# Columns of a sliding-attention and shift-MLP kernel by transposing transfers out of SBUF

## The chip, the cores and the metric

The kernel runs on one core of one Trainium2 chip. The metric is the device time of one execution in microseconds; a lower time is better. The engines are named as the profile names them: PE is TensorE's matmul, PEld its weight load, DVE is VectorE, ACT is ScalarE, POOL is GpSimd, and SP is SyncE, which issues nearly all transfers.

## The reference

The input is x of 2048 rows by 512 columns. Two branches start from its layernorm, and the second gates the first:

```python
xn = _layernorm(x)
s  = A(xn, wqkv, wo)          # 32 heads of 16; each row attends to itself and 7 earlier rows, 2 apart
g  = silu(B(xn, w1, w2, w3, w4))
out = x + s * g

# B, with F = 1376
h   = gelu(layernorm(xn) @ w1)
hs  = concat(four 128-column quarters of h, shifted by +1, -1, +2, -2 rows) @ w2
x1  = xn + hs
B   = x1 + gelu(layernorm(x1) @ w3) @ w4
```

Note that B normalises xn, which is normalised already. The kernel keeps one column-wise copy of xn for q, k and v, and reaches the second normalisation by multiplying that copy with one factor for each row.

## The kernel before, in words

**Layout.** The rows are split by parity: `xn[0]` holds the even rows and `xn[1]` the odd ones, 1024 each. There are four chunks of 512 rows, of which 0 and 1 are even and 2 and 3 odd. A chunk lies in SBUF as four tiles of 128 rows by 512 columns. A matmul over the 512 columns needs the chunk column-wise, that is with columns on the partitions: `xnT[p]` holds xn that way, `xn2T` the same times the row factors, and `x1nT` the normalised x1 ahead of w3.

**Three ways of getting columns.** `turn` (L296) makes 8 TensorE transposes for two tiles into one PSUM bank, and VectorE copies it out (L303); chunks 1, 2 and 3 take two of these each, 16 transposes a chunk. Chunk 0 goes partly by `turn_one`. `columns` (L443), ahead of w3, is the other way: after the normalisation of a chunk it writes 512x512 to `x1n_dram` (L446) and reads it back with one transposing transfer (L450).

**Row factors.** `rows2` computes 512 factors, as 128 partitions by 4. They have to stand on every partition as a row. For chunks 1 and 2, `rows2_spread` (L264) turns the 128x4 on TensorE (L266), copies it on VectorE (L268), writes it to `r2_d` (L269) and reads it back, repeated over the 128 partitions (L271), into `xn2T`. For chunks 0 and 3, `rows2_here` (L273) makes a diagonal on VectorE (L277) and multiplies it with ones on TensorE (L282). Then `scaled` (L288) multiplies the columns with them on VectorE.

**Order.** All instructions are pinned in the order of the program on each engine; nothing is moved by a planner. So the order below L489 is the schedule, and each engine, and SP's queue, takes its own instructions in that order and waits at each for what it needs. `q_all`, `k_all`, `v_pair`, `w1`, `w2` and `w3` are the projections of one chunk: 16, 16, 8, 16, 16 and 44 matmuls of width 512 (`w1` is called by halves of 8, `v_pair` by two tiles). They take PSUM in pairs of banks, three pairs in turn, and ScalarE or VectorE must have read a pair before it is written again; `k_all` has four ScalarE evictions (L354), since each key is written twice, masked for even and odd heads. `w2(c)` adds the result to xn and takes the statistics of the second layernorm (`Norm`), `columns(c)` follows, and `w3(c)` reads `x1nT`. `w2(0)` needs hT of the even chunks 0 and 1 and of the odd chunk 2, for the shifts cross from one parity to the other. Weights are loaded by SP: w3 (1376 KB) behind the first row factors, w4 behind those of chunk 2. After w3 of all chunks comes a loop of 18 attention blocks mixed with the matmuls of w4 (L878), which the change doesn't touch.

Of the kernel before, what the change touches and what calls it, by code (L numbers as in the profile page):

```python
# [8 lines left out]
AF = mybir.ActivationFunctionType  # L9
ALU = mybir.AluOpType  # L10
BF16 = mybir.dt.bfloat16
# [3 lines left out]
def ap_of(base, dims, off=0):  # L15

    return bass.AP(base.tensor, base.offset + off, dims)
# [3 lines left out]
def kernel(  # L21
# [17 lines left out]
    PE, DVE, ACT, POOL, SP = nc.tensor, nc.vector, nc.scalar, nc.gpsimd, nc.sync  # L39

    def pin(ins):

        return tc.keep_in_program_order(ins)

    P = 128
    S = 2048
    D = 512
    F = 1376
    ND = D // P
# [4 lines left out]
    CH = 512  # L54
    NCH = S // CH
# [40 lines left out]
    def single():  # L96
        cnt["s"] += 1
        return PS[:, 6 + (cnt["s"] - 1) % 2, :]
# [54 lines left out]
    m57 = const.tile([P, QB], BF16, name="m57")  # L153
    e_sb = const.tile([P, 8, 8, 16], BF16, name="e_sb")
    zero = const.tile([P, D], BF16, name="zero")

    def head_masks():
        pin(DVE.tensor_reduce(
# [36 lines left out]
    hT = [b8([P, ND, M + 2], f"hT{p}") for p in range(2)]  # L195
    kM = [kbp.tile([P, ND, MK, 2], BF16, name=f"kM{p}", tag="kM") for p in range(2)]
    v_d = [dram.tile([MK, 2, D], BF16, name=f"v_d{p}") for p in range(2)]
    r2_d = dram.tile([NCH, CH], BF16, name="r2_d")
    x1n_dram = dram.tile([S, D], BF16, name="x1n_dram")
    vst = [b4([P, 2, 2, D], f"vst{i}") for i in range(2)]  # L200


# [4 lines left out]
    def small_t(name, shape, dt=F32):  # L207
        return small.tile(shape, dt, name=name, tag=name)
# [39 lines left out]
    def rows2(c, ln):  # L248

        r2 = small_t("r2", [P, TPC])  # L250
        r2b = small_t("r2b", [P, TPC], BF16)
        eng = DVE if c == 0 else POOL
        pin(eng.tensor_tensor(out=r2, in0=ln.rstd, in1=ln.rstd, op=ALU.mult))
        pin(eng.tensor_tensor(out=r2, in0=r2, in1=ln.mv[:, :, 1], op=ALU.mult))
        if c == 0:
            pin(ACT.activation(r2, r2, AF.Sqrt, bias=eps_t[:]))
            with nc.allow_low_precision("bf16 row factors"):
                pin(DVE.reciprocal(out=r2b, in_=r2))
        else:
            rsqrt_eps(r2, r2)  # L260
            pin(POOL.tensor_copy(out=r2b, in_=r2))
        r2s[c] = r2b

    def rows2_spread(c):  # L264
        pt = single().bitcast(BF16)[0:TPC, 0:P]
        pin(PE.transpose(pt, r2s[c], ident[:]))  # L266
        t = small_t("r2t", [TPC, P], BF16)
        pin(DVE.tensor_copy(out=t, in_=pt))  # L268
        pin(SP.dma_start(out=r2_d[c].rearrange("(j q) -> j q", q=P), in_=t))  # L269
        xn2Ts[c] = b4([P, ND, CH], "xn2T")  # L270
        pin(SP.dma_start(out=xn2Ts[c][:, ND - 1, :], in_=r2_d[c : c + 1, :].to_broadcast([P, CH])))  # L271

    def rows2_here(c):  # L273

        xn2Ts[c] = t = b4([P, ND, CH], "xn2T")
        d = t[:, 0, :].rearrange("p (j q) -> p j q", q=P)
        pin(DVE.tensor_tensor(  # L277
            out=d, in0=ident.unsqueeze(1).to_broadcast([P, TPC, P]), in1=r2s[c].unsqueeze(2).to_broadcast([P, TPC, P]),
            op=ALU.mult,
        ))  # L280
        pt = single()
        pin(PE.matmul(pt, lhsT=ones_bf[:], rhs=t[:, 0, :], start=True, stop=True))  # L282
        if c == 0:
            pin(ACT.activation(t[:, ND - 1, :], pt, AF.Copy))
        else:
            pin(DVE.tensor_copy(out=t[:, ND - 1, :], in_=pt))

    def scaled(c):  # L288
        p, k = c // 2, c % 2
        t = xn2Ts[c]  # L290
        pin(DVE.tensor_tensor(
            out=t, in0=xnT[p][:, :, k * CH : (k + 1) * CH],
            in1=t[:, ND - 1, :].unsqueeze(1).to_broadcast([P, ND, CH]), op=ALU.mult,
        ))

    def turn(c, h):  # L296
        p, k = c // 2, c % 2
        i = k * TPC + 2 * h
        pt = single().bitcast(BF16).rearrange("p (a j q) -> p a j q", a=ND, j=2)
        for j in range(2):  # L300
            for dt in range(ND):
                pin(PE.transpose(pt[:, dt, j, :], xn[p][:, i + j, dt * P : (dt + 1) * P], ident[:]))  # L302
        pin(DVE.tensor_copy(  # L303
            out=xnT[p][:, :, i * P : (i + 2) * P], in_=pt.rearrange("p a j q -> p a (j q)")
        ))

    def turn_one(c, t):
        p, k = c // 2, c % 2
        i = k * TPC + t
        pt = single().bitcast(BF16)[:, 0 : ND * P].rearrange("p (a q) -> p a q", a=ND)  # L310
        for dt in range(ND):
            pin(PE.transpose(pt[:, dt, :], xn[p][:, i, dt * P : (dt + 1) * P], ident[:]))
        pin(ACT.activation(xnT[p][:, :, i * P : (i + 1) * P], pt, AF.Copy))

    def q_half(pts, lo, hi, nts=range(ND)):
        for nt in nts:
# [28 lines left out]
    def k_pad(p):  # L345
        pin(POOL.memset(kM[p][:, :, 0:8, :], 0.0))
        pin(POOL.memset(kM[p][:, :, M + 8 : MK, :], 0.0))

    def k_all(c, parts=(0, 1)):
        p, k = c // 2, c % 2  # L350
        for a in parts:
            pt = proj(c, a, wqk_sb[:, :, D : 2 * D], chunk(xnT, c))
            for e in range(2):
                pin(ACT.activation(  # L354
                    kM[p][:, 2 * a : 2 * a + 2, 8 + k * CH : 8 + (k + 1) * CH, e], pt, AF.Copy, scale=em[:, e : e + 1]
                ))
# [29 lines left out]
    def v_pair(p, t):  # L386
        pt = pair()
        for i in range(2):
            v_mm(p, t + i, pt[:, i, :])
        v_keep(p, t, 2, pt[:, 0, :])  # L390

    def v_pad(p):
        rows = v_d[p].rearrange("r e d -> (r e) d")
        pin(SP.dma_start(out=rows[0:16], in_=zero[0:16, :]))
        pin(SP.dma_start(out=rows[2 * (M + 8) : 2 * MK], in_=zero[0:4, :]))

    def w1(c, a):
        p, k = c // 2, c % 2
        pt = proj(c, a, w1_sb, xn2Ts[c])
        pin(ACT.activation(  # L400
            hT[p][:, 2 * a : 2 * a + 2, 1 + k * CH : 1 + (k + 1) * CH], pt, AF.Gelu_apprx_tanh
        ))
# [12 lines left out]
    def w2(c, order="a0 s0 a1 s1"):  # L415

        p, k = c // 2, c % 2
        x_c = x_of(c)
        ln = ln2[c] = Norm(x_c, b4([P, TPC, D], "xn3"), TPC, "l3")
        pts = []  # L420
        for h in range(TPC // 2):
            pt = pair()
            pts.append(pt)
            for j in range(2):
                m0 = k * CH + (2 * h + j) * P
                for g in range(ND):
                    pin(PE.matmul(  # L427
                        pt[:, j, :], lhsT=w2_src(p, g, m0), rhs=w2_sb[:, g, :],
                        start=(g == 0), stop=(g == ND - 1),
                    ))  # L430
        for what, i in (w for w in order.split()):
            if what == "a":
                h = int(i)
                xs = x_c[:, 2 * h : 2 * h + 2, :]
                pin(DVE.tensor_tensor(out=xs, in0=pts[h], in1=xs, op=ALU.add))  # L435
            elif what == "s":
                h = int(i)
                ln.stats(2 * h, 2 * h + 2)
            else:
                columns(c - 1)  # L440
        ln.root()

    def columns(c):  # L443
        ln = ln2[c]
        ln.apply(0, TPC)
        pin(SP.dma_start(  # L446
            out=x1n_dram[c * CH : (c + 1) * CH, :].rearrange("(i q) d -> q i d", q=P), in_=ln.dst
        ))
        x1nT = b4([P, ND, CH], "x1nT")
        pin(SP.dma_start_transpose(out=x1nT, in_=x1n_dram[c * CH : (c + 1) * CH, :]))  # L450
        x1nTs[c] = x1nT

    h3a, h3b = {}, {}
# [35 lines left out]
    for p in range(2):  # L489
        pin(POOL.memset(hT[p][:, :, 0:1], 0.0))  # L490
        pin(POOL.memset(hT[p][:, :, M + 1 : M + 2], 0.0))
        pin(POOL.memset(qT[p][:, :, M:MQ], 0.0))
    pin(POOL.memset(zero, 0.0))
    k_pad(0)
    k_pad(1)
    pin(ACT.activation(
# [32 lines left out]
    for a in range(2):  # L529
# [10 lines left out]
    v_pair(0, 2)  # L540
    k_all(0, (1,))
    v_pad(0)
    w1(0, 0)
    rows2_spread(1)
    pin(SP.dma_start(out=w3_sb, in_=B_w3.rearrange("(dt q) f -> q dt f", q=P)))
    turn(1, 0)
    turn(1, 1)
    w1(0, 1)
    l2 = Norm(x_of(2), x_of(2), TPC, "l1")
    l2.stats(0, 4)  # L550
    l2.root()
    l2.apply(0, 4)
    rows2(2, l2)
    l3 = Norm(x_of(3), x_of(3), TPC, "l1")
    l3.stats(0, 4)
    l3.root()
    scaled(1)
    q_all(1)
    k_all(1)
    v_pair(0, 4)  # L560
    l3.apply(0, 4)
    rows2(3, l3)
    v_pair(0, 6)
    rows2_spread(2)
    w1(1, 0)
    turn(2, 0)
    turn(2, 1)
    w1(1, 1)
    scaled(2)
    q_all(2)  # L570
    turn(3, 0)
    turn(3, 1)
    k_all(2)
    pin(SP.dma_start(
        out=w4_sb[:, 0 : NF - 1, :],
        in_=B_w4[0 : (NF - 1) * P, :].rearrange("(ft q) n -> q ft n", q=P),
    ))
    pin(SP.dma_start(out=w4_sb[0:FL, NF - 1, :], in_=B_w4[(NF - 1) * P : F, :]))
    rows2_here(3)
    scaled(3)  # L580
    w1(2, 0)
    w1(2, 1)
    w1(3, 0)
    w1(3, 1)
    w2(0)
    columns(0)
    v_pad(1)
    q_all(3)
# [403 lines left out]
```

## Time and profile before

| what | value |
|---|---|
| median of three runs | 199.26 us (197.72, 199.69, 199.26) |
| the profiled execution's own time | 197.26 us |
| its span in the profile | 195.5 us, mean granted clock 0.996 |
| PE busy | 185.5 us, 95% of the span |
| ACT busy | 133.3 us, 68% |
| DVE busy | 117.8 us, 60% |
| POOL busy | 19.1 us, 10% |
| transfers | 28.12 MB, mean 144 GB/s |
| start to the end of w3 | 0 to 112.4 us |
| attention blocks with w4 | 112.4 to 185 us |

The span is the time between the first and the last thing that the profiler saw; the execution's own time is 1.76 us longer. A busy share is an average over the span, so it says which engine is filled most, and a window of time says whether it is filled where the change is made. The chain that ended last is followed back from the end of the program: each piece of it is work, or a wait, that something later depended on.

### The profile page before, as it was taken

How to read it: one execution, taken by the hardware profiler on the slowest of the kernel's cores; microseconds unless marked ns; L12 is line 12 of the kernel's file. 1: busy time of each engine (PE TensorE's matmuls, PEld its weight loads, DVE VectorE, ACT ScalarE, POOL GpSimd, SP SyncE). 2: the span in 40 equal slices, each digit the busy share in tenths (PEclk: the TensorE clock that was granted, in tenths of full speed). 3: DMA queues.
4: the chain of work that ended last, by engine and by line, in shares of the span. 5: the costliest groups of instructions: out<-in, count | busy, mean ns of one | idle time of the engine just before them, and what ended most of it. 6: DMA issues, size and time to landing. Idle time of an engine off the chain costs nothing.

```text
span 195.5 us, 5255 instructions
## 1 busy us (share of the span) xinstructions
PE 185.5 (95%) x2253; PEld 91.8 (47%) x2283; DVE 117.8 (60%) x229; ACT 133.3 (68%) x151; POOL 19.1 (10%) x57
## 2 busy tenths in 40 slices
PE   7899999999999999999999999999999999999990
PEld 2474544554444444444444444445444544554540
DVE  5785767236076697494200035556487888798894
ACT  7399769649817615435656588877887876887871
POOL 3006066100002022006000000000000000000000
PEclk9999999999999999999999999999999999999998
DMA  4997480654000433752480051457565556582523
GB/s 131 339 368 239 132 282 15 218 158 157 0 0 3 136 83 109 215 107 65 110 260 0 0 162 60 157 166 232 153 216 161 137 155 215 127 247 51 171 91 126
DMA packets 33576, 28.12 MB, mean 144 GB/s; under 512 B 10760, under 2 KB 32528, under 8 KB 33552
## 3 DMA queue, kind: packets, MB, share of 16 engines
q1 hardware_dynamic: 33408, 27.71, 47.2%
q8 instruction: 18, 0.29, 0.6%
q10 hardware_dynamic: 144, 0.07, 0.1%
q14 instruction: 6, 0.05, 0.1%
HBM read 17.01 MB, written 8.67 MB: 131 GB/s over the span
## 4 chain that ended last, share of the span: by engine, by line
PE 85%; DMA 5%; DVE 4%; issue 2%; SPq 1%; ACT 1%
PE PS L469 19%; PE PS L328 19%; PE PS L764 19%; PE PS L427 5%; PE PS L811 4%; PE PS L795 4%; PE PS L652 3%; DMA wqk_sb<-in_A_wqkv_dram 3%; PE PS L626 3%; PE PS L362 3%; DMA x1nT<-x1n_dram 2%; PE PS L318 2%; PE PS L662 2%; PE PS L302 2%; DVE sg L825 2%
## 5 line engine op out<-in xcount | busy, mean ns | idle before, releaser
L469 PE MATMUL PS<-x1nT,w_sb 128*128 128x512 bf16 (+1 forms) x173 | 38.2, 379 | 0.4 <-DMA x1nT<-x1n_dram 0.3
L633 ACT ACTIVATE prob<-PS 128x1824 bf16<-128x1824 f32 x18 | 30.4, 1688 | 4.4 <-PE PS L626 3.6
L764 PE MATMUL PS<-w_sb,h3a 128*128 128x512 bf16 x112 | 29.2, 379 | 1.9 <-issue 1.7
L475 ACT ACTIVATE h3a<-PS 128x1024 bf16<-128x1024 f32 x16 | 16.4, 1024 | 21.0 <-PE PS L469 19.1
L777 DVE TENSOR_TENSOR xn<-PS,xn 128x512 bf16<-128x512 f32 x15 | 10.3, 686 | 32.0 <-PE PS L764 31.8
L469 PEld LDWEIGHTS <-w_sb 128*128 128x128 bf16 (+1 forms) x176 | 17.5, 100 | 20.9 <-issue 0.7
L328 PE MATMUL PS<-xnT,wqk_sb 128*128 128x512 bf16 x109 | 25.0, 379 | 0.2
L354 ACT ACTIVATE kM<-PS,em 128x1024 bf16<-128x1024 f32 x16 | 20.8, 1404 | 3.2 <-PE PS L328 3.2
L638 DVE TENSOR_TENSOR prob<-prob,maskb 128x1824 bf16<-128x1824 bf16 x18 | 19.8, 1102 | 1.8 <-ACT prob L633 1.8
L764 PEld LDWEIGHTS <-h3a 128*128 128x128 bf16 x128 | 11.3, 97 | 13.4 <-issue 1.2
L328 PEld LDWEIGHTS <-wqk_sb 128*128 128x128 bf16 x112 | 10.9, 98 | 12.8
L435 DVE TENSOR_TENSOR xn<-PS,xn 128x1024 bf16<-128x1024 f32 x8 | 9.6, 1213 | 11.3 <-PE PS L427 11.3
L811 PE MATMUL PS<-wo_sb,oT 128*128 128x512 bf16 (+1 forms) x68 | 15.5, 366 | 0.0
L328 PE MATMUL PS<-xn2T,w_sb 128*128 128x512 bf16 x62 | 14.6, 379 | 0.1
L427 PE MATMUL PS<-w_sb,hT 128*128 128x512 bf16 x63 | 14.4, 379 | 0.1
L821 ACT ACTIVATE sg<-PS 128x512 bf16<-128x512 f32 (+1 forms) x17 | 9.6, 572 | 6.1 <-PE PS L811 6.1
L764 PE MATMUL PS<-w_sb,h3b 128*128 128x512 bf16 (+1 forms) x44 | 12.8, 380 | 0.8 <-issue 0.8
L339 ACT ACTIVATE qT<-PS 128x1024 bf16<-128x1024 f32 x8 | 8.1, 1024 | 7.6 <-PE PS L328 7.6
L373 ACT ACTIVATE vst<-PS 128x512 bf16<-128x512 f32 (+1 forms) x12 | 8.8, 743 | 3.5 <-ACT sig L784 2.3
L221 DVE BATCH_NORM_STATS2 l1s<-xn 128x6 f32<-128x512 bf16 x16 | 10.1, 680 | 1.6 <-DMA xn<-in_A_x_dram 1.6
L400 ACT ACTIVATE hT<-PS 128x1024 bf16<-128x1024 f32 x8 | 8.1, 1031 | 3.8 <-PE PS L328 3.8
L221 DVE BATCH_NORM_STATS2 l3s<-xn 128x6 f32<-128x512 bf16 x16 | 10.2, 682 | 0.2
(105 smaller groups left out, 229.2 us busy)
## 6 DMA issues: line engine op xcount, KB each, us to landing
ring<-v_d SPq DMA_DIRECT2D x18, 256.0 KB, 3.3
v_d<-vst SPq DMA_DIRECT2D x16, 256.0 KB, 2.7
x1n_dram<-xn SPq DMA_DIRECT2D x4, 512.0 KB
xo<-in_A_x_dram SPq DMA_DIRECT2D x8, 256.0 KB, 4.1
ring<-rec_d SPq DMA_DIRECT2D x4, 456.0 KB, 4.7
out_dram<-xo SPq DMA_DIRECT2D x7, 256.0 KB
xn<-in_A_x_dram SPq DMA_DIRECT2D x6, 256.0 KB, 7.9
w_sb<-in_B_w_dram SPq DMA_DIRECT2D x1, 1376.0 KB
```

Source lines behind the costliest of these rows:

```text
L221: pin(DVE.bn_stats(out=self.st[:, j, :], in_=self.src[:, j, :]))
L328: pin(PE.matmul(pt[:, b, :], lhsT=w[:, dt, nt * P : (nt + 1) * P], rhs=rhs[:, dt, :], start=(dt == 0), stop=(dt == ND - 1),))
L354: pin(ACT.activation(kM[p][:, 2 * a : 2 * a + 2, 8 + k * CH : 8 + (k + 1) * CH, e], pt, AF.Copy, scale=em[:, e : e + 1]))
L427: pin(PE.matmul(pt[:, j, :], lhsT=w2_src(p, g, m0), rhs=w2_sb[:, g, :], start=(g == 0), stop=(g == ND - 1),))
L435: pin(DVE.tensor_tensor(out=xs, in0=pts[h], in1=xs, op=ALU.add))
L469: pin(PE.matmul(pt[:fs, ft % 2, :], lhsT=w3_sb[:, dt, ft * P : ft * P + fs], rhs=x1nT[:, dt, :], start=(dt == 0), stop=(dt == ND - 1),))
L475: pin(ACT.activation(t[:, o : o + 2, :], pt, AF.Gelu_apprx_tanh))
L633: pin(ACT.activation(pr, S_ps[:, :, 0 : ND * NQ], AF.Exp, scale=SCALE))
L638: pin(DVE.tensor_tensor(out=f, in0=f, in1=maskb[:], op=ALU.min))
L764: pin(PE.matmul(pt, lhsT=h3_of(c, ft)[:fs, jj * P : (jj + 1) * P], rhs=w4_sb[:fs, ft, :], start=(ft == 0), stop=(ft == NF - 1 and silu < 2),))
L777: pin(DVE.tensor_tensor(out=x_i, in0=pt, in1=x_i, op=ALU.add))
L811: pin(PE.matmul(pt[:, 0:W], lhsT=oT[p][:, dt, i * P : (i + 1) * P], rhs=wo["sb"][:, dt, c], start=(dt == 0), stop=(dt == ND - 1),))
```

## The change

The columns of chunks 2 and 3 no longer come by `turn` but by `turn_dma`: four transposing transfers for each chunk, 128x512 each, straight from xn in SBUF to `xnT` in SBUF. `columns` does the same with the normalised tiles: four transposing transfers out of SBUF for a chunk in place of a write to DRAM and one transposing transfer back.

The row factors of chunks 1, 2 and 3 are turned by VectorE: the 128x4 factors stand in a zeroed 128x32 tile (`r2p`), VectorE turns it in blocks of 32x32, and the result is written to DRAM as 128 pieces of 32 elements, so that the first 512 elements are the row. Write and read are two functions now, called at different places of the order; chunk 3 goes this way too, and no longer by `rows2_here`.

In the order, `l3.apply` and `rows2(3)` move ahead of the value projections, the load of w3 moves from behind the first row factors to behind the last, and `w2(0)` moves ahead of `w1(3, 1)`.

```diff
+    r2p = const.tile([P, NCH, 32], BF16, name="r2p")
...
-    r2_d = dram.tile([NCH, CH], BF16, name="r2_d")
-    x1n_dram = dram.tile([S, D], BF16, name="x1n_dram")
+    r2_d = dram.tile([NCH, 32 * P], BF16, name="r2_d")
...
             rsqrt_eps(r2, r2)
-            pin(POOL.tensor_copy(out=r2b, in_=r2))
+            r2b = r2p[:, c, :]
+            pin(POOL.tensor_copy(out=r2b[:, 0:TPC], in_=r2))
...
-    def rows2_spread(c):
-        pt = single().bitcast(BF16)[0:TPC, 0:P]
-        pin(PE.transpose(pt, r2s[c], ident[:]))
-        t = small_t("r2t", [TPC, P], BF16)
-        pin(DVE.tensor_copy(out=t, in_=pt))
-        pin(SP.dma_start(out=r2_d[c].rearrange("(j q) -> j q", q=P), in_=t))
+    def rows2_write(c):
+        t = small_t("r2t", [P, 32], BF16)
+        pin(DVE.transpose(out=t, in_=r2s[c]))
+        pin(SP.dma_start(out=ap_of(r2_d[c], [[32, P // 32], [P, 32], [1, 32]]), in_=t))
+
+    def rows2_read(c):
         xn2Ts[c] = b4([P, ND, CH], "xn2T")
-        pin(SP.dma_start(out=xn2Ts[c][:, ND - 1, :], in_=r2_d[c : c + 1, :].to_broadcast([P, CH])))
+        pin(SP.dma_start(out=xn2Ts[c][:, ND - 1, :], in_=r2_d[c : c + 1, 0:CH].to_broadcast([P, CH])))
...
+    def turn_dma(c):
+        p, k = c // 2, c % 2
+        for t in range(TPC):
+            i = k * TPC + t
+            pin(SP.dma_start_transpose(out=xnT[p][:, :, i * P : (i + 1) * P], in_=xn[p][:, i, :]))
...
         ln.apply(0, TPC)
-        pin(SP.dma_start(
-            out=x1n_dram[c * CH : (c + 1) * CH, :].rearrange("(i q) d -> q i d", q=P), in_=ln.dst
-        ))
         x1nT = b4([P, ND, CH], "x1nT")
-        pin(SP.dma_start_transpose(out=x1nT, in_=x1n_dram[c * CH : (c + 1) * CH, :]))
+        for t in range(TPC):
+            pin(SP.dma_start_transpose(out=x1nT[:, :, t * P : (t + 1) * P], in_=ln.dst[:, t, :]))
...
     v_pad(0)
+    rows2_write(1)
     w1(0, 0)
-    rows2_spread(1)
-    pin(SP.dma_start(out=w3_sb, in_=B_w3.rearrange("(dt q) f -> q dt f", q=P)))
     turn(1, 0)
     turn(1, 1)
+    rows2_read(1)
     w1(0, 1)
...
     l2.apply(0, 4)
+    turn_dma(2)
     rows2(2, l2)
...
     l3.root()
+    rows2_write(2)
     scaled(1)
     q_all(1)
     k_all(1)
+    l3.apply(0, 4)
+    turn_dma(3)
+    rows2_read(2)
+    rows2(3, l3)
+    rows2_write(3)
     v_pair(0, 4)
-    l3.apply(0, 4)
-    rows2(3, l3)
     v_pair(0, 6)
-    rows2_spread(2)
+    rows2_read(3)
+    pin(SP.dma_start(out=w3_sb, in_=B_w3.rearrange("(dt q) f -> q dt f", q=P)))
     w1(1, 0)
-    turn(2, 0)
-    turn(2, 1)
     w1(1, 1)
     scaled(2)
     q_all(2)
-    turn(3, 0)
-    turn(3, 1)
     k_all(2)
+    scaled(3)
...
-    rows2_here(3)
-    scaled(3)
     w1(2, 0)
     w1(2, 1)
     w1(3, 0)
+    w2(0)
     w1(3, 1)
-    w2(0)
     columns(0)
```

More of the change, by code (lines that the diff above doesn't have):

```diff
@@ L250, in rows2 @@
         r2 = small_t("r2", [P, TPC])
-        r2b = small_t("r2b", [P, TPC], BF16)
         eng = DVE if c == 0 else POOL
@@ L256, in rows2 @@
             pin(ACT.activation(r2, r2, AF.Sqrt, bias=eps_t[:]))
+            r2b = small_t("r2b", [P, TPC], BF16)
             with nc.allow_low_precision("bf16 row factors"):
@@ L282, in rows2_here @@
         pin(PE.matmul(pt, lhsT=ones_bf[:], rhs=t[:, 0, :], start=True, stop=True))
[L283 to L286, printed above, removed]
+        pin(ACT.activation(t[:, ND - 1, :], pt, AF.Copy))
     def scaled(c):
@@ L493 @@
     pin(POOL.memset(zero, 0.0))
+    pin(POOL.memset(r2p, 0.0))
     k_pad(0)
```

## The prediction

> **What bounds the kernel now.** I read the page's busy shares first, then the chain that ended last in order of time, then busy time by windows, then the timeline of the SP queue, since the change puts its transfers there.
>
> ```profile
> PE 185.5 (95%) x2253; PEld 91.8 (47%) x2283; DVE 117.8 (60%) x229; ACT 133.3 (68%) x151; POOL 19.1 (10%) x57
> ```
>
> TensorE is busy for 95% of the span. An average hides stages, so the stage that is changed is read alone, in windows of 5 us (columns: length, then busy us of each engine, granted clock, DMA share, GB/s):
>
> ```profile
> 30.00:35.00 5.00, 4.95 (x24) 2.15 (x23) 3.07 (x11) 5.00 (x5) 3.97 (x7) 1.00 0.00 0
> 35.00:40.00 5.00, 5.00 (x37) 2.75 (x35) 1.29 (x2) 2.50 (x4) 0.02 (x1) 1.00 0.65 213
> 40.00:45.00 5.00, 4.95 (x36) 2.75 (x35) 2.63 (x4) 2.70 (x3) 0.00 (x0) 1.00 0.74 232
> ```
>
> TensorE has no more than 0.05 us free in any of the three, at full clock, while VectorE and the transfers have room. So in this stage a TensorE instruction that goes away is worth its place in the row, and other work counts only if it makes TensorE wait. The chain says what the instructions to be removed hold (start, length, what):
>
> ```profile
> 20.25 0.15 PE PS L266
> ...
> 33.48 0.15 PE PS L266
> 33.63 1.83 PE PS L328 x8
> 35.46 0.89 PE PS L302 x16
> 36.36 4.53 PE PS L328 x21
> ...
> 41.54 0.89 PE PS L302 x16
> 42.43 3.45 PE PS L328 x16
> 45.88 0.22 PE PS L282
> 46.10 3.02 PE PS L328 x14
> ```
>
> L302 x16 is one chunk's `turn`, L266 a row factor's turn, L282 the matmul of `rows2_here(3)`. Sixteen 512-wide matmuls take 3.45 us, 0.216 each; I use that pitch below. The transfers, on the SP queue (start, issue time):
>
> ```profile
> 37.01 0.47 SPq L269 DMA_DIRECT2D r_d<-r2t  x1
> 39.26 0.34 SPq L271 DMA_DIRECT2D xn2T<-r_d  x1
> ...
> 63.17 0.39 SPq L446 DMA_DIRECT2D x1n_dram<-xn  x1
> 66.16 2.20 SPq L450 DMA_TRANSPOSE x1nT<-x1n_dram  x1
> ```
>
> One transposing transfer of 512x512 out of DRAM holds SP for 2.20 us here; over the four of them it is 1.31 at least and 1.98 in the median. The chain gives it 4.51 us from issue to the matmul that it releases (66.16 to 70.67), so 2.31 us after SP is free. TensorE itself waited 0.27 us for it, since 13.8 us of other matmuls lie ahead.
>
> **What is removed.** 32 transposes: 2 x 0.89 = 1.78 us. Two row turns: 2 x 0.15 = 0.30. The matmul of L282: 0.22. Together 2.30 us of TensorE. On VectorE four copies of 0.64, one product of 0.68, one cast of 0.69 and two copies of 0.21 go, and three turns of 128x32 come (no row has one; the 4x128 copy took 0.21, a 128x512 pass 0.43, so 0.2 to 0.43 each, I take 0.2, the smaller tile); that engine is 60% busy and none of it leads the chain there, so nothing is counted.
>
> **What is added: transposing transfers out of SBUF.** There are 8 for the columns of chunks 2 and 3 and 16 for the columns ahead of w3, each 128x512, in place of 4 of 512x512 and 4 writes to DRAM. No row shows one that reads SBUF. Call x what one holds SP. The bounds: a quarter of the shortest issue, 1.31 / 4 = 0.33 us, if it goes by size; the longest whole issue, 2.20 us, if it goes by instruction. I take a quarter of the median, 0.5 us, because three plain issues above with sizes from 1 to 512 KB took 0.34 to 0.47 us, so the fixed part is small beside 1.98. Landing: 2.31 us after the issue.
>
> With x = 0.5: the normalised tiles of chunk 2 are ready at 27.8 (VectorE's L237 ran 26.41 to 27.79), so its columns land at 27.8 + 0.5 + 2.3 = 30.6. `q_all(2)` would start at 36.36 + 8 x 0.216 - 0.30 - 0.89 = 36.9: covered by 6 us. Chunk 3's tiles are ready at 34.2, needed past 54: covered. Row factors of chunk 2: behind `turn_dma(3)` SP is free at 34.7, the broadcast took 3.11 us (39.26 until `scaled(2)` started at 42.37), `scaled(2)` 1.23, so 39.0; `w1(2, 0)` wants it at 46.10 - 2.30 = 43.8: covered by 4.8. Chunk 3's row read stands behind one more write and four value stores (2.52 us of SP): 34.7 + 0.34 + 0.47 + 2.52, landing and scaling by 42.4, wanted at 47.3. The row write is now 128 pieces of 64 bytes; the nearest row is `rec_d`, also 128 pieces, for which SP waited 2.1 us at most, against 1.8 for the old row write: at most 0.3 us more, within every cover named. Chunk 1's factors have theirs by some 27, and VectorE reaches `scaled(1)` at 30.4, behind statistics.
>
> Columns ahead of w3: call T the end of w2(0)'s matmuls (56.48 now). The first normalised tile is ready at T + 5.6 and the last at T + 6.7, so the columns land at T + 9.5 without the DRAM write. w3(0) now has w1(3, 1), q, k, w2(1) and w2(2) ahead of it, 72 matmuls or 15.5 us: covered by 6 us, and the present wait of 0.27 goes. Chunks 1 to 3 lose their DRAM write (SP waited 11.9 us for the four) and are wanted later still.
>
> **What is moved.** w3's load goes behind the last row read, to about 40, with w4's load right behind it: 2.7 MB at the 280 GB/s of the window 25 to 30 is 10 us, done by 50 against w3(0) near 67. `w2(0)` ahead of `w1(3, 1)`: it reads the halves that `w1(2, 0)` wrote, whose gelu follows the key evictions. These (ACT L354, 44.20 to 49.37) end 3.49 us after k_all(2)'s matmuls, and w1(3, 0), which takes that PSUM pair, would now start after 16 x 0.216 = 3.45 us: a wait of about 0.1 us, a small cost.
>
> **Sum.** 2.30 + 0.27 - 0.1 = 2.45 us. The profiled execution took 197.26 us (span 195.5 and 1.76 around it), so 194.8. The median of the three runs shown, 199.26, stands 2.0 above the profiled one; on that scale 196.8.
>
> **Weighing a rule.** The Trainium skill, "VectorE: DVE Perf Modes", section "The three transpose paths", gives a 128x128 transpose as 390 ns on TensorE and 1309 ns by DMA, and its rules table prefers TensorE where PSUM will do. Here 16 such TensorE transposes took 0.89 us, 56 ns each in a row, and one transposing transfer carried 16 blocks in 4.51 us; at 1309 ns for each block, one after the other, the transfer would have taken 21 us, so the trace disagrees with a serial reading. It speaks against this change only where the transfer is late, which is the third rival.
>
> **Rivals.**
>
> *A. SP becomes the bound: slower.* Transfers out of SBUF cost by instruction, not by size. From 26.8, when chunk 2's first tile is ready, SP issues eight of them and a row write of 0.47 before it reads chunk 2's factors, so `scaled(2)` ends at 26.8 + 8x + 0.47 + 3.11 + 1.23 = 31.6 + 8x against 43.8. TensorE starts to wait from x = 1.52, and the gain is gone at x = 1.83. At the median 1.98 the wait is 3.65, the columns ahead of w3 add T + 5.6 + 4 x 1.98 + 2.3 - (T + 15.5) = 0.3, net +1.5: 200.8. At 2.20 it is 5.4 + 1.2 - 2.45 = +4.2: 203.4. For it: SP's issue of a transposing transfer is four to six times that of a plain one, so it does work for each piece, and a source across partitions may have more. Against: if it goes by piece, a quarter of the pieces costs a quarter.
>
> *B. Same.* x lies between 1.6 and 1.8, and the 2.45 us are nearly eaten by the wait for chunk 2's factors: at x = 1.75 the wait is 1.8, net -0.6, 198.6.
>
> *C. The transfers land one after the other, each as long as the whole one, 4.51 us.* A chunk then takes 18 us. Chunk 2 lands at 44.8 against 36.9, and the four chunks ahead of w3 come every 18 us where w3 takes 9.5: waits of 7.9, 0.5, 7.6, 5.1, 8.5 and 8.5, net +36: 235. Against it: transfers in flight overlap elsewhere in this trace (three ring loads issued within 1.39 us).
>
> **How the numbers follow.** The forecast holds 0.68; A 0.22, B 0.06, C 0.04. One per cent, about what a measurement of this kernel can tell from no change, is 2.0 us, and the forecast of 2.45 is past it by little: I put 0.10 of the 0.68 within 1%. So faster 0.58, same 0.10 + 0.06 = 0.16, slower 0.26. The forecast's own range is 195.5 to 198.0 (a gain between 1.3 and 3.7: waits that I count at 0.27 and 0.1 off by some tenths, and the spread of the runs). To hold 8 in 10 the range takes in B and A up to x of about 2.08, 202.0.
>
> **What would show it.** Right: no L302 rows past 30 us, `q_all(2)` near 36.9, w1(2, 0) near 43.8, w3(0) near 68.2 with no TensorE idle put down to a DMA, the span near 193.0, and SP issues of the new transfers of about 0.5 us. Wrong: issues over 1.5 us, VectorE's `scaled(2)` or `scaled(3)` waiting for `r_d` past 44, or TensorE waiting for `xnT` or `x1nT`; each such wait comes straight off the 2.45.

## The result, and the profile after

Over 20 runs each the changed kernel took 199.29 us in the median (197.46 to 202.76) and the kernel before 197.74 (196.43 to 200.14). The ratio is 1.006, with a 95% interval of 1.0036 to 1.0083; six executions of the changed kernel with a granted clock of 0.987 to 0.992 are left out of it, which is why it is a little under that of the medians. So the change cost 0.6%, 1.2 us, where 2.45 us less were forecast. The profiled execution has a span of 197.0 us against 195.5.

TensorE's line on the page of the changed kernel looks like the old one, 1.3 us more although there are 35 transposes and matmuls fewer in the program (the counts leave out records that a trace misses):

```profile
PE 186.8 (95%) x2248; PEld 90.1 (46%) x2248; DVE 114.2 (58%) x224; ACT 133.3 (68%) x151; POOL 19.3 (10%) x58
```

Two places make up the difference. The first is the stage that was changed. The windows of 5 us there (length, busy us of PE, PEld, DVE, ACT and POOL with their instructions, clock, DMA share, GB/s):

```profile
35.00:40.00 5.00, 5.00 (x25) 2.25 (x23) 0.00 (x0) 2.91 (x3) 0.00 (x0) 1.00 0.47 99
40.00:45.00 5.00, 5.00 (x25) 2.26 (x24) 1.23 (x1) 4.29 (x4) 0.00 (x0) 1.00 0.83 243
45.00:50.00 5.00, 3.12 (x15) 1.28 (x14) 1.23 (x1) 3.67 (x4) 0.00 (x0) 1.00 0.93 312
```

TensorE is full until 45 and then loses 1.88 us. The chain of the changed kernel there (start, length, what):

```profile
32.91 7.08 PE PS L333 x32
...
41.39 0.62 SPq L382
...
42.10 5.19 DMA xn2T<-r_d
...
47.47 1.24 DVE xn2T L290
...
48.76 1.90 PE PS L333 x8
50.66 3.45 PE PS L432 x16
```

The 32 matmuls of w1(1, 0), w1(1, 1) and q of chunk 2 run without a transpose between them, as was wanted. But then the chain leaves TensorE, which goes on with other matmuls until 46.88: it goes to SP's value stores (L382), to the read of chunk 3's row factors, 5.19 us from issue to landing, and to `scaled(3)` on VectorE. The view of TensorE's waits, over the whole span (total us, times, longest), says what that costs:

```profile
PE PS L333 <- DVE xn2T L290: 1.9, 1, 1.9
PE PS L657 <- issue: 1.5, 1, 1.5
...
PE PS L667 <- issue: 0.8, 1, 0.8
```

The first line is that wait. The other two are the second place, and it lies 95 us later, in the attention blocks, which no edit touched: TensorE stood for 1.46 and 0.78 us ("issue": it waited for nothing that the profile shows). In the timeline of block 8 (start, length, engine, line; the bracket is the idle time before):

```profile
142.32 0.40 PE L631 MATMUL PS<-qT,kM 32*128 32x57 bf16 x32
142.66 0.39 PE L657 MATMUL PS<-prob,ring 128*32 128x57 bf16 x28
144.50 0.21 PE L657 MATMUL PS<-prob,ring 128*32 128x57 bf16 x4 [1.46 <-issue]
144.54 0.38 PE L667 MATMUL PS<-prob,den_st 128*32 128x114 bf16 x16
```

It stops in the middle of 32 equal matmuls, after the 28th, with its data there. The page of before has an "issue" line too, 2.5 us in 16 pieces ahead of L764; that one is an artefact, since 16 of that line's 128 matmuls are missing from that trace, and the gaps stand where they ran.

To compare kernels I split each trace in two: stage 1 from the first matmul with w_qk (8.94 us before, 8.55 after) to the first with w4 (112.24 and 111.15), and stage 2 from there to the end of the span. Before: 103.30 and 83.26 us. After: 102.60 and 85.85. So stage 1 gained 0.70 of the forecast 2.45 (the wait of 1.88 is what it lacks, to within 0.13), and stage 2 lost 2.59. With 0.39 us of earlier start this is the 1.5 us between the spans.

### The profile page after: what moved, and what is told of

Same layout as the page of the kernel before. It is cut to its first block, busy times and chain, and to the rows that moved or that the text cites. A ratio compares the mean times of both kernels' runs of the same rounds, so it can differ in the third digit from the quotient of the medians.

```text
span 197.0 us, 5262 instructions
## 1 busy us (share of the span) xinstructions
PE 186.8 (95%) x2248; PEld 90.1 (46%) x2248; DVE 114.2 (58%) x224; ACT 133.3 (68%) x151; POOL 19.3 (10%) x58
## 4 chain that ended last, share of the span: by engine, by line
PE 85%; ACT 4%; DVE 4%; DMA 3%; issue 2%; SPq 0%; DVEq 0%; ACTq 0%
PE PS L769 21%; PE PS L472 19%; PE PS L333 15%; PE PS L432 5%; PE PS L816 4%; PE PS L367 4%; PE PS L800 4%; PE PS L657 3%; PE PS L631 3%; DMA xn2T<-r_d 3%; ACT kM L359 3%; PE PS L141 2%; PE PS L667 2%; PE PS L323 2%; DVE xo L836 2%
## 5 line engine op out<-in xcount | busy, mean ns | idle before, releaser
L769 PE MATMUL PS<-w_sb,h3a 128*128 128x512 bf16 x128 | 32.7, 380 | 0.0
L769 PE MATMUL PS<-w_sb,h3b 128*128 128x512 bf16 (+1 forms) x48 | 13.5, 381 | 0.0
L290 DVE TENSOR_TENSOR xn2T<-xnT,xn2T 128x2048 bf16<-128x2048 bf16 x4 | 4.8, 1206 | 11.6 <-DMA v_d<-vst 6.8
```

Source lines behind the costliest of these rows:

```text
L769: pin(PE.matmul(pt, lhsT=h3_of(c, ft)[:fs, jj * P : (jj + 1) * P], rhs=w4_sb[:fs, ft, :], start=(ft == 0), stop=(ft == NF - 1 and silu < 2),))
```

## The experiments

Theory F says that the pauses in stage 2 are late fetches of TensorE's own instructions. The profile counts 17 pieces of 0.28 MB in all, 16 KiB each, on the queue called "instruction". The trace of the changed kernel has 4532 TensorE instructions: 2248 matmuls, as many weight loads, and 36 semaphore and drain instructions, which the listings leave out. From the first pause to the second it has 768 of them, three times 256 (the expectations below have 766, without the semaphore instructions). The Trainium skill, "Runtime: NRT & Kernel Launch", section "Instruction fetch mechanics", says that each engine's instructions come in 16 KiB blocks of 256 over a queue of its own; the spacing agrees. It also calls the cost of crossing a block "mostly hidden"; the 1.46 us here disagrees. Theory Q says that the wait in stage 1 comes from the place of one read in SP's queue.

**The changed kernel again (`after_again`).** No edit.

> The changed kernel once more, nothing edited. In its first profile TensorE paused for 1.46 us in the middle of values of block 8 (after the 28th of 32 matmuls of L657) and for 0.78 us in block 12 (after the 10th of 16 of L667), with nothing that it waited for; from the first w4 matmul to the end of the span the kernel took 85.7 us against 83.1 before. Theory F: these are late fetches of TensorE's own instructions, which come in blocks of 256 (the two places lie 766 instructions apart, nearly 3 x 256), and since the block limits are fixed by the program the pauses come again at the same two places, with sizes of 0.5 to 2 us, and the stage takes 85 to 86 us. Rival N: they are chance of that one execution; then they are absent or elsewhere, and the stage takes 83 to 84 us. In both, TensorE waits 1.9 us for scaled(3) near 47 us again.

Ratio 1.0045 (1.0009 to 1.008). Both pauses came at the same two places:

```profile
144.82 0.39 PE L657 MATMUL PS<-prob,ring 128*32 128x57 bf16 x28
146.39 0.21 PE L657 MATMUL PS<-prob,ring 128*32 128x57 bf16 x4 [1.18 <-issue]
...
160.94 0.32 PE L667 MATMUL PS<-prob,den_st 128*32 128x114 bf16 x10
161.76 0.28 PE L667 MATMUL PS<-prob,den_st 128*32 128x114 bf16 x6 [0.51 <-issue]
```

Same matmuls, the 28th and the 10th, with other sizes (1.18 and 0.51); the wait for `scaled(3)` was 2.2 us. Stage 2 took 85.26 us, at a granted clock of 0.985. The places belong to the program, and chance alone (N) is out.

**70 instructions more ahead of everything (`after_pad35`).**

```diff
-    for i in range(10):
-        pin(PE.matmul(PS[:, 6 + i % 2, :], lhsT=ones_bf[:], rhs=<512 columns of ones>, ...))
+    for i in range(45):
+        pin(PE.matmul(PS[:, 6 + i % 2, 0:114], lhsT=ones_bf[:], rhs=ones_bf[:, 0:114], ...))
```

> The changed kernel, but with the 10 warm-up matmuls of 512 columns at the start made into 45 of 114 columns: the same time at the start, and 70 TensorE instructions more, so that the attention stage has its instructions at the same places in the blocks of 256 as in the kernel before. Theory F (late instruction fetches): the stage from the first w4 matmul to the end goes back from 85.7 to about 83.1 us, and the ratio to the kernel before goes from 1.006 to about 0.995. Rival D (the stage is slower for its data: value rows, ring loads or v_d placed or timed otherwise): the stage stays at 85 to 86 us and the ratio at 1.006.

The warm-up lasted 4.45 us as before. Stage 2 took 83.23 us and had no pause. The total did not follow in full: ratio 1.0005 (0.9971 to 1.0038) where 0.995 was expected. In that profile TensorE waited 2.5 us for `scaled(3)` rather than 1.9, which is part of it; the rest is not explained by this profile, whose execution took 196.85 us where the median of the twelve is 198.78. The stage speaks for F and against D.

**The row read ahead of the value stores (`after_read3`).**

```diff
     rows2_write(3)
+    rows2_read(3)
     v_pair(0, 4)
     v_pair(0, 6)
-    rows2_read(3)
```

> The changed kernel with chunk 3's row read (L273) issued right behind its row write, ahead of the four value stores and so further ahead of the loads of w3 and w4. Theory Q (the 1.9 us that TensorE waits for scaled(3) come from the read's place in SP's queue and from its landing of 5.2 us beside the weight loads, against 3.1 to 3.6 us for the other reads): the read lands by about 44.5, the wait is gone, w3(0) starts 1.9 us sooner and w3 ends near 109.4 instead of 111.3; total 1 to 1 per cent less than the changed kernel, ratio about 0.996. Rival S (SP's eight transposing issues of 1.3 us set it, whatever the order behind them): the read moves by less than 1 us and the wait stays over 1 us, ratio 1.006. Theory F adds that the attention stage keeps its two pauses, since no TensorE instruction is added.

Ratio 0.9932 (0.9902 to 0.9962). SP's queue, first of the changed kernel and then of this one (start, issue time):

```profile
38.52 0.53 SPq L269 DMA_DIRECT2D r_d<-r2t  x1
39.15 2.85 SPq L382 DMA_DIRECT2D v_d<-vst  x4
42.10 0.57 SPq L273 DMA_DIRECT2D xn2T<-r_d  x1
42.71 0.45 SPq L574 DMA_DIRECT2D w_sb<-in_B_w_dram  x1
```

```profile
39.28 0.53 SPq L269 DMA_DIRECT2D r_d<-r2t  x1
41.61 0.33 SPq L273 DMA_DIRECT2D xn2T<-r_d  x1
41.99 2.59 SPq L382 DMA_DIRECT2D v_d<-vst  x4
44.63 0.71 SPq L574 DMA_DIRECT2D w_sb<-in_B_w_dram  x1
```

The read was issued only 0.5 us sooner, as S had it, and 1.2 sooner counted from the first w_qk matmul (9.29 here). But `scaled(3)` started 3.0 us behind the issue (44.62) in place of 5.4 (47.47). The wait was gone, and stage 1 took 100.79 us, 1.8 less: S is out, and Q holds in that the read's place sets the wait. The landing, 2.4 us shorter, would have covered the wait of 1.88 by itself; the earlier issue, 1.2 us, would not. The pauses stayed at the same places (after 27 and 10 matmuls, 0.82 and 0.31 us), stage 2 84.52. The ratio is below the 0.996 expected, in part for these shorter pauses.

Why the landing was long, this edit can't say by itself, for it moved the read away from w3's load, as Q has it, and also ahead of the value stores. The kernel before has two reads with a weight load close behind and no store in flight:

```profile
22.48 0.35 SPq L271 DMA_DIRECT2D xn2T<-r_d  x1
22.88 0.43 SPq L545 DMA_DIRECT2D w_sb<-in_B_w_dram  x1
...
39.65 0.86 SPq L574 DMA_DIRECT2D w_sb<-in_B_w_dram  x1
```

L545 is w3's load, 0.40 us behind chunk 1's read, which landed 3.86 us after its issue. L574 is w4's load, 0.39 us behind chunk 2's read of 39.26, which landed in 3.02. In `after_read3` the value stores, 1 MB, come 0.38 us behind the read, and it landed in 2.99. So a bulk transfer close behind a read is not enough for 5.2. In the changed kernel the stores stand ahead: the last of them landed at 44.27, and the read's first packet moved at 43.81, 1.7 us after the issue of 42.10, where it took 1.0 us in the other three. By these rows, as an estimate, w3's load accounts for some 0.9 us of the landing (3.86 less 3.02) and the stores ahead for some 1.3 (5.19 less 3.86); no run moves one without the other.

**Both edits (`after_read3_pad35`).**

> Both edits: the row read ahead of the value stores, and 70 TensorE instructions more at the start. If theories F and Q both hold, the stage before w4 ends near 109.4 us and the attention stage takes 83.1: the forecast gain is there, ratio about 0.986. If only Q holds, 0.996; if only F, 0.995; if neither, 1.006.

Ratio 0.9826 (0.9787 to 0.9866), median 194.83 us; stage 1 100.97, stage 2 83.59 with one pause of 0.5 at another place. The forecast gain is there: 2.1 us between the two profiled executions (197.26 and 195.13), and 3.4 by the ratio. Why the ratio shows more than the profiles is not explained.

**The pauses put into the kernel before (`before_pad93`).**

```diff
-    for i in range(10):   # 512 columns each
+    for i in range(103):  # 50 columns each
```

> The kernel before, with its 10 warm-up matmuls of 512 columns made into 103 of 50 columns: 186 TensorE instructions more, so that the attention stage lies in the blocks of 256 as it does in the changed kernel (70 fewer, which is 186 more less one block). Theory F (late fetches at block limits): the pauses of the changed kernel come up here, in values of block 8 and in the denominators of block 12, 0.3 to 1.5 us each, and the stage from the first w4 matmul to the end takes 84.5 to 86 us in place of 83.3, with no other edit. Rival C (the pauses belong to the changed kernel's transfers): no pauses, 83.3 us. The total may also carry a later start, since 103 small matmuls may last some us longer than 10 wide ones; the stage decides.

Stage 2 went from 83.26 to 85.46 us with nothing else edited, and the pauses came in blocks 8 and 12:

```profile
144.98 0.21 PE L659 MATMUL PS<-prob,den_st 128*32 128x114 bf16 x1
146.28 0.39 PE L659 MATMUL PS<-prob,den_st 128*32 128x114 bf16 x15 [1.09 <-issue]
...
160.81 0.38 PE L659 MATMUL PS<-prob,den_st 128*32 128x114 bf16 x16
162.29 1.04 PE L761 MATMUL PS<-w_sb,h3a 128*128 128x512 bf16 x4 [1.10 <-issue]
```

They stand five or six matmuls later than in the changed kernel: in block 8 after the first of the denominators (L659 here) instead of the 28th of the values. The semaphore instructions account for it: the changed kernel has 11 more of them ahead of the attention, so it is 59 instructions shorter there and not 70. Counted with them from the start of the trace, the first instruction behind a pause is the same in its block of 256 in all nine pauses of five kernels (`after`, `after_again`, `after_read3`, this one, and the one pause of `after_read3_pad35`): 193 instructions and a whole number of blocks lie ahead of it. So all nine lie a whole number of blocks of 256 apart, as block limits do. C is out: this kernel has none of the transfers out of SBUF. Its ratio is 1.0278 (1.0224 to 1.0332). The profiled execution, 200.43 us, is 3.2 above that of the kernel before, of which 2.2 are stage 2 and 1.1 a new wait for `xn2T` in stage 1; the other three took 202.0 to 204.8 us, and that I can't place.

**Half a block (`read3_pad64`).** `after_read3` with 74 warm-up matmuls of 69 columns.

> The changed kernel with the early row read, and 64 warm-up matmuls more (74 of 69 columns for 10 of 512): 128 TensorE instructions, half a block of 256. Theory F: the pauses at the 28th matmul of values in block 8 and at the 10th of the denominators in block 12 are gone, since the block limits now lie half a block away, in the scores of blocks 9 and 12, in the denominators of block 10, in the values of block 13; any pause lies at one of these. With the transfers busiest in blocks 7 and 8, where no limit follows closely, I expect 0.5 us of pauses or less and a stage of 83 to 83.6 us, ratio about 0.985. Rival W (what counts is the narrower warm-up or the mere number of instructions, in proportion): 128 instructions do more than 70 did, and the stage goes below 83.

Stage 2 took 83.17 us and blocks 8 and 12 took 3.81 and 3.89 us (5.45 and 4.88 in the changed kernel); block 16 alone was long, 4.37 against 3.88 before. Ratio 0.9857 (0.9819 to 0.9895). None of the places named had a pause. 128 instructions did no more than 70, and in `before_pad93` 186 made the stage longer, so W is out.

The stage by place in the blocks of 256 (to within the 11 semaphore instructions), over all kernels:

| place of the attention code | kernels and their stage 2, us |
|---|---|
| as in the changed kernel | `after` 85.85, `after_again` 85.26 (clock 0.985), `after_read3` 84.52, `before_pad93` 85.46 |
| as in the kernel before | `before` 83.26, `after_pad35` 83.23, `after_read3_pad35` 83.59, and of the kernels below `r3_turns` 82.98, `r3p35_dramcol` 82.89, `before_col4` 82.95, `r3p35_w2late` 82.68 |
| half a block off the changed kernel | `read3_pad64` 83.17 |

**Why these two limits (from the traces of `after` and `after_pad35`).** In the changed kernel the 16 transfer engines are full ahead of the pause (columns as above: length, PE, PEld, DVE, ACT, POOL, clock, DMA share, GB/s), first `after`, then `after_pad35`:

```profile
139.00:141.00 2.00, 2.00 (x48) 1.03 (x32) 0.24 (x1) 2.00 (x3) 0.00 (x0) 1.00 0.97 231
141.00:142.30 1.30, 1.30 (x7) 0.39 (x4) 1.03 (x2) 0.62 (x2) 0.00 (x0) 1.00 1.12 384
```

```profile
139.00:141.00 2.00, 2.00 (x86) 1.26 (x86) 0.95 (x2) 1.41 (x2) 0.00 (x0) 1.00 0.87 231
141.00:142.30 1.30, 1.30 (x8) 0.58 (x7) 0.25 (x1) 1.30 (x3) 0.00 (x0) 1.00 0.90 201
```

The piece of TensorE's instructions nearest ahead of the pause began to move at 142.07 in `after`, beside 113 data packets in 0.3 us, and at 136.92 in `after_pad35`, ahead of the busiest stretch. So both kernels are busy with data there (231 GB/s in the first window of both, 384 against 201 in the second); the one fetches its next block in the rush and the other ahead of it.

All nine pauses look alike in this. The piece came late: it began to move 1.4 to 3.5 us after TensorE had passed the limit before, and over that time the transfer engines' share was 0.95 to 1.11. And TensorE went on 1.27 to 1.55 us after the end of that piece. At every other limit of the attention stage, in the eight traces that lack no matmul of it, the piece had ended 1.56 us or more ahead, and TensorE did not pause. The piece itself was not slowed, for it took 0.95 to 1.21 us, where all pieces of these traces took 0.88 to 1.87; it started late. That the rush delays the start is read from these times; an experiment that thins out the data in blocks 6 to 8 was not made.

**What one transposing issue costs (`before_col4`).** The kernel before, with the transfer ahead of w3 in four of 128 rows, still out of DRAM.

```diff
-        pin(SP.dma_start_transpose(out=x1nT, in_=x1n_dram[c * CH : (c + 1) * CH, :]))
+        for t in range(TPC):
+            pin(SP.dma_start_transpose(out=x1nT[:, :, t * P : (t + 1) * P],
+                                       in_=x1n_dram[c * CH + t * P : c * CH + (t + 1) * P, :]))
```

> The kernel before, with its transposing transfer of 512x512 out of DRAM ahead of w3 made into four of 128x512, still out of DRAM. It prices the term that was mis-sized, what one transposing issue holds SP for: 1.98 us for 512x512 out of DRAM, 1.30 for 128x512 out of SBUF. Theory I (it goes by instruction, with a fixed part near 1 us): 1.1 to 1.4 us each. Theory B (it goes by the source: a source in SBUF costs more for each piece): 0.4 to 0.6 us each, a quarter of the whole.

The source lines, for the transfers of `after` out of SBUF, of `before_col4` out of DRAM, and of `before`:

```profile
L453 SPq DMA_TRANSPOSE x1nT<-xn x16: 1189/1219/1417, 59.9 to 92.9; - x16
```

```profile
L451 SPq DMA_TRANSPOSE x1nT<-x1n_dram x16: 1196/1258/1307, 65.8 to 102.1; - x16
```

```profile
L450 SPq DMA_TRANSPOSE x1nT<-x1n_dram x4: 1308/1980/2202, 66.2 to 94.9; - x4
```

1.22 us out of SBUF, 1.26 out of DRAM, 1.98 for four times the rows: the source makes no difference to speak of. By the medians (1.98 - 1.26) / 3 = 0.24 us goes with each 128 rows, so about 1.0 us of it is fixed; that split is an estimate, since one of the four large issues took 1.31. Theory I holds. The one execution of this kernel took 200.43 us; it is used for its issues alone.

**Single parts undone on the best kernel (`r3p35_dramcol`, `r3_turns`, `r3p35_w2late`).** The columns ahead of w3 by DRAM again; the columns of chunks 2 and 3 by `turn` again; `w2(0)` behind `w1(3, 1)` again. The first:

> The best of the kernels so far (changed kernel, row read ahead of the value stores, 70 more TensorE instructions; ratio 0.983), with the columns ahead of w3 again by a write to DRAM and one transposing transfer back. Theory T (only TensorE's instructions count, and the columns are covered by 15.5 us of matmuls either way): within 0.3 us, ratio 0.982 to 0.985. Rival K (transfers out of SBUF in place of DRAM are a good part of the gain, by less traffic): slower by 1 us or more, ratio 0.988 or above.

194.80 us against 194.83; ratio 0.9867 (0.9844 to 0.9889). That is just outside what T gave (0.982 to 0.985) and short of K's 0.988, and the interval holds values of both; the stages decide for T, since stage 1 took 100.77 us against 100.97 and stage 2 had no pause. The second, with its edit:

```diff
-    turn_dma(2)
...
-    turn_dma(3)
...
     w1(1, 0)
+    turn(2, 0)
+    turn(2, 1)
     w1(1, 1)
     scaled(2)
     q_all(2)
+    turn(3, 0)
+    turn(3, 1)
     k_all(2)
```

> The same best kernel, with the columns of chunks 2 and 3 again by 32 TensorE transposes and four VectorE copies at their old places, and the warm-up 13 matmuls wide instead of 45 so that the attention stage keeps its place in the blocks of 256. Theory T: the 32 transposes cost what the chain showed, 1.78 us, ratio about 0.992. Rival H (TensorE's instructions were hidden in other waits): less than 0.7 us, ratio 0.986 or below.

Ratio 0.9929 (0.9906 to 0.9952), 195.97 us; stage 1 took 102.56 us against 100.77 in the run with DRAM columns and 100.97 in the best kernel, so 1.6 to 1.8 us: T. The third:

> The best kernel with w2(0) behind w1(3, 1) again, as in the kernel before: the normalisation of chunk 0 starts 1.73 us later against w3(0). Theory T (the columns out of SBUF land some 12 us after w2(0)'s matmuls, and 13.8 us of other matmuls follow): no wait for x1nT, the same time within 0.3 us, ratio 0.982 to 0.986. Rival E (the earlier place is needed, since four issues of 1.22 us take the slack): TensorE waits 0.5 to 1.5 us ahead of w3(0), ratio 0.988 or above.

Ratio 0.9837 (0.9806 to 0.9868), 194.68 us; stage 1 took 101.01. No wait for `x1nT`: T again, and E is out.

## Why the prediction was wrong, point by point

- **The removed TensorE work was sized right.** Counted from the first w_qk matmul, w1(2, 0) came 2.44 us sooner (46.10 - 8.94 against 43.27 - 8.55) for the 2.30 of the sum, and `r3_turns` gives 1.6 to 1.8 us of it back for the 1.78 of the transposes.
- **The term that was mis-sized: x.** I took 0.5 us for what one transposing issue holds SP; it was 1.22 in the median, for the columns of chunks 2 and 3 as for those ahead of w3, inside the bounds of 0.33 and 2.20 and about halfway between the two theories (0.5 by size, 1.98 by instruction). I reasoned from plain issues that the fixed part is small; for a transposing issue it is about 1.0 us, by the estimate above. It stayed under rival A's limit of 1.52: `scaled(2)` ended at 42.7 and TensorE took w1(2, 0) at 43.27 without waiting, so A's wait for chunk 2 did not come.
- **The step that failed first: chunk 3's row read "landing and scaling by 42.4, wanted at 47.3".** It was issued at 42.10 rather than 38.0, of which x makes 3.1 us (SP was free behind `turn_dma(3)` at 37.8 and not at 34.7) and longer issues behind that the rest. And it landed in 5.19 us, not in the 3.11 that I took from chunk 2's read of before. That read had a weight load 0.39 us behind it too, but no store in flight ahead of it; here four value stores were still moving when the read was issued, and w3's load came 0.61 us behind. I had counted what the stores hold SP for, and asked whether w3 comes in time, but not what either does to the landing of the read. `scaled(3)` ended at 48.7, and 1.88 us of the gain went. (The prediction had named a wait of `scaled(3)` for `r_d` past 44 as a sign of being wrong.) Of the two errors the landing is the one that failed: with the late issue and a landing of 3.11, `scaled(3)` would have ended at 42.10 + 3.11 + 1.23 = 46.4, ahead of the 46.88 at which TensorE wanted it.
- **The step that failed by more: a term put at nothing.** The sum has no term for the attention blocks, which no edit touches, and so carries stage 2 at its old length. It became 2.59 us longer, because 59 instructions fewer ahead of it put the limits of TensorE's instruction blocks at other matmuls, and two of these blocks came late. None of the three rivals has this. That the place of the code sets it is shown by taking it away (`after_pad35`, `after_read3_pad35`) and by putting it into the old kernel (`before_pad93`). That the data traffic makes these blocks late is argued from times and not shown.
- **Right, though without weight for the time.** The columns ahead of w3 were covered and no wait for a transfer stood ahead of w3(0); by DRAM or out of SBUF they give the same time, and so does `w2(0)` at either place. The 0.27 us that I booked for them is within what these runs can tell apart.
- **Rival C did not happen.** The four transfers of chunk 2 were issued in 5.22 us from 26.19 on, and q_all(2), at 36.4, did not wait for `xnT`.
- **The range.** The measured 199.29 lies inside the 195.5 to 202.0 of the prediction, but by luck: the upper part of that range was for a wait for chunk 2's factors, which did not happen, and the scale of the three runs (199.26) was 1.5 us above the median of 20 (197.74). On that scale the forecast would have been 195.3.

## What to carry to other kernels

When work is taken off the engine that sets the time, price the replacement by instruction as well as by byte, and look at what is still in flight ahead of each small transfer that something waits for, and at what is issued just behind it: a row read behind 1 MB of stores and 0.6 us ahead of a weight load landed in 5.2 us, and the same read ahead of the stores in 3.0. And when a stage that was not touched gets longer, look for idle time in the middle of a run of equal instructions: an edit moves all the code behind it, and a few instructions of padding show whether the place of the code, and not the edit, is what is paid for.

## What the runs showed that I had not expected

- TensorE paused for 0.3 to 1.5 us at limits of its instruction blocks, where a block of 256 is used up in 4 to 7 us and the transfer engines were full (share 0.95 to 1.11) before the next block moved. It went on 1.27 to 1.55 us after the end of that transfer. The effect on stage 2 was 0.9 to 2.6 us, as large as the whole forecast gain.
- A transposing issue of 128x512 holds SP for 1.22 us from SBUF and 1.26 from DRAM, one of 512x512 for 1.98: by estimate about 1.0 us, and 0.24 us for each 128 rows.
- VectorE's turn of 128x32 took 0.18 to 0.21 us in the changed kernel's trace, for the 0.2 taken.
